# Masking by a product, plain float32 products for eight chunks, and value means on TensorE, in a fused attention and two-layer expert kernel

## The chip, the cores and the metric

The kernel runs on one core of a Trainium2 chip. The metric is the device time of one execution in microseconds (us); the time of a kernel is the median of its runs.

## What is computed

Three stages follow one another. The first is attention over two batches, eight heads, 768 positions and 64 channels per head. Each position sees the neighbours nearer than 16 positions and, besides, one summary per block of 32 positions (24 of them): the elementwise maximum of the keys and the mean of the values. The second stage is a dense layer pair with an ELU between, 512 to 2048 to 512. The third sends each of the 1536 tokens to one of eight experts.

```python
k_sum = k.reshape(B, H, nb, block, D).max(axis=3)
v_sum = v.reshape(B, H, nb, block, D).mean(axis=3)
scores_l = scale * np.matmul(q, k.transpose(0, 1, 3, 2))
mask_l = np.abs(pos[:, None] - pos[None, :]) < window
scores_s = scale * np.einsum('bhsd,bhnd->bhsn', q, k_sum) + np.log(block)
scores_all = np.concatenate([np.where(mask_l, scores_l, -1e9), scores_s], axis=-1)
...
h = x @ w_in
g = np.where(h > 0.0, h, np.exp(np.minimum(h, 0.0)) - 1.0)
x = g @ w_out
...
out[mask] = gate_w[mask, None] * eom[mask, e, None] * (np.maximum(x[mask] @ w1[e], 0.0) @ w2[e])
```

## The kernel before

**Units and blocks.** The 1536 tokens are 24 attention units of 64 positions; units 0 to 11 are batch 0, the rest batch 1. The units form four blocks of 8, 4, 6 and 6 units, so 512, 256, 384 and 384 tokens (`UNITS`, `TBS`). The dense layers run block by block. Within a block the 2048 hidden features are 16 chunks of 128 (`NF`). Chunk c of a block consists of `mm_h` (twelve products into one PSUM bank), `elu`, and two chunks later `mm_y`, which adds its share to the block's output banks, one per 128 tokens (`TPB`).

**One attention unit.** Four pairs of heads share a unit. `scores` (line 303) makes, for each pair, a product of 128 rows (64 queries of two heads) by 120 columns (24 summaries and 96 neighbours). `maxes` (line 312) adds the mask to each pair's scores and takes the row maximum in one VectorE instruction of its own kind per pair (line 319), followed by a read of the accumulator; the masked scores lie in SBUF as `e`. `at1b` takes the exponentials on ScalarE, from `e` to `e`, with the maximum as bias. In units 3 and 5 (`EXD`) `less_max` subtracts the maximum first, on GpSimd in unit 3 and on VectorE in unit 5, and one exponential serves all four pairs. `norm`, `turn` (four transposes), `weighted` (the product with the values), `x_hi` and `at5` follow and leave the unit's columns of x in a high and a low float32r part. The scores of units 0 to 7 take a bank of the pool with tag `y`, later ones the single bank `S`; transposes and weighted sums of the later units share the single bank `T`.

**Split products.** Float32 accuracy is kept by splitting operands into two float32r parts: three products (high by high, high by low, low by high) replace one. For `mm_y`, `split_w` (line 169) splits the weights with a ScalarE cast and a VectorE subtraction (line 176), and `split_g` (line 438) does the same to the ELU's output (`gh`, line 445, and `gl`, line 446). The first `C3` chunks of block 0 do without: there one plain float32 product is made per output bank.

**Weights.** The dense weights arrive as raw 64-bit words, 16 chunks of each matrix. `conv_t` (lines 138, 139, VectorE), `conv_r` (line 127, ScalarE) and `conv_f` (line 146, GpSimd) turn a piece into float32; pieces of `w_in` are split afterwards by `conv_h` (line 152, ScalarE) and `conv_l` (line 157, mostly VectorE). Each piece holds two buffers of the five-buffer pool `stg` meanwhile. All 32 conversions belong to block 0, two to a chunk in program order.

**Value means of batch 1.** Eight pieces of the transposed values are loaded into `stg` buffers (line 217), and GpSimd adds 32 neighbours in a tree of five steps per piece (`tree`, lines 233 to 237). `vsums2` (line 243) then transposes the 24 means on TensorE, through the bank `T`, and the result goes into the first 24 rows of every value tile of batch 1 (`v_pad`, line 255). For batch 0, `mean_v0` does this with products from the start.

**What sets the order.** The start, units 0 to 7 and the first chunks, follows the list `START`, in which each letter is a step and each number a unit or a chunk; what is loaded first follows `ORDER`. Behind it the program writes steps with due half-steps (`at(...)`), and the compiler's scheduler interleaves them on each engine by its own estimate of times; the expert stage has a planner of its own. On the chip each engine takes its instructions in that fixed order.

```python
for n, name in enumerate(("kT", "vT")):
    for p in range(NP):
        for hf in range(2):
            hs = SUM0 + 4 * n + p
            at(hs - 1, self.load_sum, name, p, hf)
            at(hs, self.red_sum, name, p, hf)
at(SUM0 + 9, self.vsums2)
...
self.mm_h(j, c, TB // 2 if j == 0 and c in self.half else 0)
conv()
self.split_w(j, c)
if i:
    self.split_g(*steps[i - 1])
self.elu(j, c)
```

Of the kernel before, what the change touches and what calls it, by code (L numbers as in the profile page):

```python
# [79 lines left out]
class Prog:  # L80
# [134 lines left out]
    def load_sum(self, name, p, hf):  # L215
        t = self.stg.tile([128, S // 2], F32, tag="stg", name="kst")
        self.nc.sync.dma_start(t, self.a[name][:, p, hf * S // 2:(hf + 1) * S // 2])
        self.st[name, p, hf] = t

    def red_sum(self, name, p, hf):  # L220
        nc = self.nc
        t = self.st.pop((name, p, hf)).rearrange("p (n w) -> p n w", w=32)
        n0, n1 = hf * NB // 2, (hf + 1) * NB // 2
        if name == "kT":
            nc.vector.tensor_reduce(self.ks[1][:, p, n0:n1], t, axis=AX.X, op=ALU.max)
            return
        if p == 0 and hf == 0:
# [2 lines left out]
        if p == NP - 1 and n1 == NB:  # L230
            nc.gpsimd.tensor_scalar(self.vs, self.vs, 1.0 / 32.0, None, op0=ALU.mult)

    def tree(self, p, n0, n1, t):
        nc = self.nc
        for w in (16, 8, 4, 2):
            nc.gpsimd.tensor_tensor(t[:, :, :w], t[:, :, :w], t[:, :, w:2 * w], op=ALU.add)
        nc.gpsimd.tensor_tensor(self.vs[:, p, n0:n1].unsqueeze(2), t[:, :, 0:1], t[:, :, 1:2], op=ALU.add)
# [1258 lines left out]
```

## Time and profile before

| | before |
|---|---|
| runs | 567.45, 567.43, 567.11 us |
| median | 567.43 us |
| profiled execution | 567.62 us, its span 565.4 us |
| TensorE busy in the span | 531.3 us (94%) |
| VectorE, ScalarE, GpSimd busy | 375.8, 317.3, 137.0 us |
| mean granted TensorE clock | 0.977 of full |

The span is the time from the first to the last instruction that the trace records; some 2.2 us of the execution lie outside it. PE is TensorE's products, PEld its weight loads, DVE is VectorE, ACT ScalarE, POOL GpSimd, SP the engine that issues most transfers. The attention start fills the first 40 us, block 0 the stretch from there to about 173 us (its last products overlap with the first of block 1), blocks 1 to 3 the stretch to about 380 us, the experts the rest. A float32 product stands in the trace as two matmul records, a float32r or bfloat16 product as one.

### The profile page before, as it was taken

How to read it: one execution, taken by the hardware profiler on the slowest of the kernel's cores; microseconds unless marked ns; L12 is line 12 of the kernel's file. 1: busy time of each engine (PE TensorE's matmuls, PEld its weight loads, DVE VectorE, ACT ScalarE, POOL GpSimd, SP SyncE). 2: the span in 40 equal slices, each digit the busy share in tenths (PEclk: the TensorE clock that was granted, in tenths of full speed). 3: DMA queues.
4: the chain of work that ended last, by engine and by line, in shares of the span. 5: the costliest groups of instructions: out<-in, count | busy, mean ns of one | idle time of the engine just before them, and what ended most of it. 6: DMA issues, size and time to landing. Idle time of an engine off the chain costs nothing. (4 is left out here: it accounts for less than half of the span.)

```text
span 565.4 us, 9609 instructions
## 1 busy us (share of the span) xinstructions
PE 531.3 (94%) x3089; PEld 422.0 (75%) x3089; DVE 375.8 (66%) x978; ACT 317.3 (56%) x774; POOL 137.0 (24%) x180
## 2 busy tenths in 40 slices
PE   8777997889869999999999999999999999999995
PEld 4465675667659889988888988987888665675884
DVE  7999999999966887687656779785841100444510
ACT  5774666756447877776566755673232222555620
POOL 3656245325980000000000000431431111100001
PEclk9999998999889999999999999998999999999999
DMA  9999543242133130310100101531077989494611
GB/s 289 329 362 394 187 156 124 86 116 79 43 105 122 48 94 16 108 57 14 48 2 0 57 1 39 170 128 57 7 206 278 373 280 362 168 373 130 234 69 40
DMA packets 39003, 81.33 MB, mean 144 GB/s; under 512 B 4128, under 2 KB 9632, under 8 KB 38945
## 3 DMA queue, kind: packets, MB, share of 16 engines
q1 hardware_dynamic: 36624, 73.30, 38.4%
q0 software_dynamic: 2320, 7.34, 3.7%
q8 instruction: 26, 0.43, 0.3%
q14 instruction: 33, 0.26, 0.2%
HBM read 103.70 MB, written 6.55 MB: 195 GB/s over the span
## 5 line engine op out<-in xcount | busy, mean ns | idle before, releaser
L422 PE MATMUL h<-xh,wi 128*128 128x384 f32 (+2 forms) x528 | 145.3, 343 | 3.0 <-ACT wi L152 1.9
L465 PE MATMUL y<-wsp,gh 128*128 128x512 f32 x368 | 116.0, 403 | 6.1 <-DVE wsp L176 5.9
L422 PEld LDWEIGHTS h<-xh,wi 128*128 128x128 f32 x528 | 95.3, 192 | 11.5 <-ACT wi L152 2.4
L422 PE MATMUL h<-xl,wi 128*128 128x384 f32 (+2 forms) x264 | 89.2, 338 | 0.0
L465 PEld LDWEIGHTS y<-wsp,gh 128*128 128x128 f32 x368 | 66.7, 190 | 20.1 <-DVE wsp L176 7.6
L465 PE MATMUL y<-wsp,gl 128*128 128x512 f32 x184 | 69.8, 399 | 0.0
L1153 DVE TENSOR_TENSOR holdl<-S,holdh 128x512 fp32r<-128x512 f32 x22 | 15.2, 689 | 72.1 <-ACT holdh L1149 53.7
L1121 PE MATMUL h<-w2s,holdh 128*128 128x512 f32 x176 | 60.9, 407 | 0.0
L1164 PE MATMUL y<-w2s,holdh 128*128 128x512 f32 x176 | 59.1, 398 | 0.0
L422 PEld LDWEIGHTS h<-xl,wi 128*128 128x128 f32 x264 | 50.8, 192 | 3.9 <-issue 0.2
L176 DVE TENSOR_TENSOR wsp<-wo,wsp 128x512 fp32r<-128x512 f32 x62 | 47.4, 765 | 8.1 <-ACT wsp L175 7.5
L175 ACT CAST wsp<-wo 128x512 fp32r<-128x512 f32 x62 | 38.2, 619 | 21.6 <-PE y L465 14.5
L434 DVE SCALAR_TENSOR_TENSOR elt<-ele,elt 128x384 f32<-128x384 f32 (+2 forms) x64 | 38.7, 605 | 16.9 <-ACT ele L432 16.5
L445 ACT CAST gh<-elp 128x384 fp32r<-128x384 f32 (+2 forms) x62 | 31.5, 508 | 30.6 <-DVE elp L435 22.4
L431 ACT ACTIVATE elt<-h 128x384 f32<-128x384 f32 (+2 forms) x64 | 31.3, 490 | 24.1 <-PE h L422 20.0
L435 DVE SCALAR_TENSOR_TENSOR elp<-elt,elp 128x384 f32<-128x384 f32 (+2 forms) x64 | 41.9, 655 | 3.5
L446 DVE TENSOR_TENSOR gl<-elp,gh 128x384 fp32r<-128x384 f32 (+2 forms) x62 | 37.4, 602 | 7.7 <-ACT gh L445 7.3
L465 PEld LDWEIGHTS y<-wsp,gl 128*128 128x128 f32 x184 | 34.4, 189 | 7.6 <-DVE gl L446 0.6
L1121 PEld LDWEIGHTS h<-w2s,holdh 128*128 128x128 f32 x176 | 33.8, 192 | 8.4 <-issue 0.8
L1164 PEld LDWEIGHTS y<-w2s,holdh 128*128 128x128 f32 x176 | 33.0, 188 | 8.4 <-issue 1.6
L336 ACT ACTIVATE e<-e,nb 128x120 f32<-128x120 f32 x88 | 33.7, 388 | 8.7 <-DVE nb L324 8.6
L1121 PE MATMUL h<-w2s,holdl 128*128 128x512 f32 x88 | 35.0, 398 | 0.0
(290 smaller groups left out, 948.0 us busy)
## 6 DMA issues: line engine op xcount, KB each, us to landing
wo<-in_w SPq DMA_DIRECT2D x9, 2048.0 KB
wo<-in_w SPq DMA_DIRECT2D x18, 1024.0 KB
ri<-in_w_in SPq DMA_DIRECT2D x16, 512.0 KB
ro<-in_w_out SPq DMA_DIRECT2D x16, 512.0 KB
wo<-in_w SPq DMA_DIRECT2D x32, 256.0 KB
w2p<-in_w SPq DMA_DIRECT2D x32, 256.0 KB
w2q<-in_w SPq DMA_DIRECT2D x24, 256.0 KB
q<-in_q SPq DMA_DIRECT2D x18, 256.0 KB
```

Of the source, the lines that this page charges most:

```text
L175: nc.scalar.copy(w[:, 0], f)
L176: nc.vector.tensor_tensor(w[:, 1], f, w[:, 0].bitcast(F32), op=ALU.subtract)
L336: nc.scalar.activation(e[:, p], e[:, p], AF.Exp, bias=nb[:, p:p + 1], scale=0.125, accum_out=sm[:, p:p + 1])
L422: nc.tensor.matmul(h, lhsT=w[:, wl, k * 128:k * 128 + 128], rhs=x[:, k, a:b], start=(n == 0), stop=(n == 11))
L431: nc.scalar.activation(t, h, AF.Tanh, scale=0.5)
L434: nc.vector.scalar_tensor_tensor(t, e, 1.0, t, op0=ALU.add, op1=ALU.mult)
L435: nc.vector.scalar_tensor_tensor(p, t, 0.0, p, op0=ALU.min, op1=ALU.add)
L445: nc.scalar.copy(gh, p)
L446: nc.vector.tensor_tensor(gl, p, gh.bitcast(F32), op=ALU.subtract)
L465: nc.tensor.matmul(self.y[j][t], lhsT=gx[:, sl], rhs=wx, start=(c == 0 and n == 0), stop=(c == NF - 1 and n == len(ops) - 1))
L1121: nc.tensor.matmul(self.h[s, hf], lhsT=x[:, k], rhs=w, start=(n == 0), stop=(n == 11))
L1164: nc.tensor.matmul(self.y2[s], lhsT=g[:, ks], rhs=w, start=(i == 0 and n == 0), stop=(i == 7 and n == 2))
```

## The change

There are three parts. **Mask.** The mask becomes the first product of a unit's accumulation group: a bfloat16 product of `mq` (two 64 by 64 identities side by side, and three rows of ones) with `mk` (the mask's rows, and the constant of the summaries in three bfloat16 parts), 480 columns wide; the four score products add to it. VectorE then takes one plain maximum over the four pairs, `at1b` reads the scores from PSUM, and `less_max` is on VectorE for both units. The bank of the scores is now held until the exponentials are done. The mask and the constants are loaded ahead of three of the four key tiles; `mask_parts` builds `mq` on GpSimd and `mk` on VectorE. **Second product.** `C3` goes from 2 to 8: eight chunks of block 0 have plain float32 products in `mm_y` and no splits. Their ELU output takes the buffers of `gh` and `gl`. **Value means.** Six pieces of the untransposed values of batch 1 are loaded, and each is reduced by four float32 products with four columns (`blk`) into the bank `T`, which ScalarE copies to `vs`.

```diff
-C3 = 2
+C3 = 8
-ORDER = "k3 k1 k2 k0 q2 q0 q5 q3 v7 c0 n1 c1 n4 n0 q1 ...
+ORDER = "k3 c1 c0 k1 k2 k0 q2 q0 q5 q3 v7 n1 n4 n0 q1 ...
-EXP = (0, 1, 2, 3, 4, 6, 7)
...
     def load_c(self, i):
+        nc.sync.dma_start(self.mask[:MK], self.a["mask"])
+
+    def mask_parts(self):
+        nc = self.nc
+        self.mq = self.const.tile([128, 128], BF16, name="mq")
+        self.mk = self.const.tile([128, 3, NK], BF16, name="mk")
+        nc.gpsimd.memset(self.mq[UQ:MK], 1.0)
+        for h in range(2):
+            nc.gpsimd.tensor_copy(self.mq[:UQ, h * UQ:h * UQ + UQ], self.ident[:UQ, :UQ])
+        nc.vector.tensor_copy(self.mk[:MK], self.mask[:MK])
...
+    def load_v1(self, i):
+        t = self.stg.tile([128, 512], F32, tag="stg", name="vn1")
+        self.nc.sync.dma_start(t, self.a["vn1"][i])
+        self.st["v", i] = t
+
+    def mean_v1(self, i):
+        t = self.st.pop(("v", i))
+        if i == 0:
             self.vs = self.sm.tile([128, NP, NB], F32, tag="vs", name="vs", bufs=1)
-        self.tree(p, n0, n1, t)
...
+        T = self.bank(self.psa, "T")
+        for p in range(NP):
+            self.nc.tensor.matmul(T[:, 4 * p:4 * p + 4], lhsT=t[:, p * 128:p * 128 + 128], rhs=self.blk[:, 20:24], start=True, stop=True)
+        self.nc.scalar.copy(self.vs[:, :, 4 * i:4 * i + 4], T[:, :16].rearrange("p (a n) -> p a n", a=NP))
...
+        m = self.mk[:MK, 0 if u % UPB == 0 else (2 if u % UPB == UPB - 1 else 1)]
+        nc.tensor.matmul(ps, lhsT=self.mq[:MK], rhs=m.unsqueeze(1).to_broadcast([MK, NP, NK]), start=True, stop=False)
         for p in range(NP):
-            nc.tensor.matmul(ps[:, p], lhsT=s["q"][:, p], rhs=k, start=True, stop=True)
+            nc.tensor.matmul(ps[:, p], lhsT=s["q"][:, p], rhs=k, start=False, stop=(p == NP - 1))
...
-        for p in range(NP):
-            nc.vector.tensor_tensor_reduce(e[:, p], ps[:, p], m, scale=1.0, scalar=-3.0e38, op0=ALU.add, op1=ALU.max, accum_out=mx[:, p:p + 1])
+        nc.vector.tensor_reduce(mx, ps, axis=AX.X, op=ALU.max)
...
-            nc.scalar.activation(e[:, p], e[:, p], AF.Exp, bias=nb[:, p:p + 1], scale=0.125, accum_out=sm[:, p:p + 1])
+            nc.scalar.activation(e[:, p], ps[:, p], AF.Exp, bias=nb[:, p:p + 1], scale=0.125, accum_out=sm[:, p:p + 1])
...
-        (self.nc.gpsimd if u in EXP else self.nc.vector).tensor_tensor(s["e"], s["e"], s["mx"].unsqueeze(2).to_broadcast([128, NP, NK]), op=ALU.subtract)
+        self.nc.vector.tensor_tensor(s["e"], s["ps"], s["mx"].unsqueeze(2).to_broadcast([128, NP, NK]), op=ALU.subtract)
...
+        pool, tag = (self.gp, "gh" if c % 2 else "gl") if j == 0 and c < C3 else (self.el, "p")
+        p = pool.tile([128, TB], F32, tag=tag, name="elp")[:, :TBS[j]]
...
+        for i in range(6):
+            hs = SUM0 + 4 + 2 * i // 3
+            at(hs - 1, self.load_v1, i)
+            at(hs, self.mean_v1, i)
```

The scheduler also places other work anew. In the rows below line numbers of the changed kernel are larger by 14 to 19; a number behind `ri`, `ro` or `wi` is the weight chunk, `cv_t` a piece being converted, and each `elp` written from `elt` ends one chunk's ELU.

The first place is VectorE in chunk 7 of block 0, before, from the conversion of `ro10` to the end of the ELU (`elp_1224`) and one row on:

```order
L138 TENSOR_SCALAR cv_t_1209<-ro10_956 128x512
L446 TENSOR_TENSOR gl_1219<-elp_1146,gh_1218 128x512
L434 SCALAR_TENSOR_TENSOR elt_1222<-ele_1223,elt_1222 128x512
L324 TENSOR_SCALAR nb_1305<-mx_1300 128x4
L139 SCALAR_TENSOR_TENSOR cv_t_1209<-ro10_956,cv_t_1209 128x512
L138 TENSOR_SCALAR cv_t_1242<-ri11_1019 128x512
L435 SCALAR_TENSOR_TENSOR elp_1224<-elt_1222,elp_1224 128x512
L157 TENSOR_TENSOR wi10_1206<-cv_t_1175,wi10_1206 128x512
```

The same place in the changed kernel, from shortly behind the ELU of chunk 6 on (`elp_1146` ends chunk 7's):

```order
L153 SCALAR_TENSOR_TENSOR cv_t_1138<-ro10_932,cv_t_1138 128x512
L367 TENSOR_SCALAR rr_1110<-sm_1044 128x4
L152 TENSOR_SCALAR cv_t_1156<-ri11_980 128x512
L368 RECIPROCAL rr_1110<-rr_1110 128x4
L153 SCALAR_TENSOR_TENSOR cv_t_1156<-ri11_980,cv_t_1156 128x512
L375 TENSOR_TENSOR e_1039<-e_1039,rr_1110 128x480
L171 TENSOR_TENSOR wi10_1135<-cv_t_1104,wi10_1135 128x512
L152 TENSOR_SCALAR cv_t_1187<-ro11_982 128x512
L450 SCALAR_TENSOR_TENSOR elt_1144<-ele_1145,elt_1144 128x512
L152 TENSOR_SCALAR cv_t_1224<-ri12_984 128x512
L153 SCALAR_TENSOR_TENSOR cv_t_1187<-ro11_982,cv_t_1187 128x512
L451 SCALAR_TENSOR_TENSOR elp_1146<-elt_1144,elp_1146 128x512
```

`gl` is gone from the chunk, and four pieces are converted ahead of its ELU's end (`ro10`, `ri11`, `ro11`, and the first step of `ri12`), where the last one begun had been `ri11`.

The second place is VectorE behind the ELU of chunk 12 before (`elp_1602`), where the last two pieces are converted:

```order
L435 SCALAR_TENSOR_TENSOR elp_1602<-elt_1600,elp_1602 128x512
L138 TENSOR_SCALAR cv_t_1550<-ri15_1191 128x512
L176 TENSOR_TENSOR wsp_1665<-wo_101,wsp_1665 128x512
L139 SCALAR_TENSOR_TENSOR cv_t_1550<-ri15_1191,cv_t_1550 128x512
L446 TENSOR_TENSOR gl_1669<-elp_1602,gh_1668 128x512
L434 SCALAR_TENSOR_TENSOR elt_1672<-ele_1673,elt_1672 128x512
L435 SCALAR_TENSOR_TENSOR elp_1674<-elt_1672,elp_1674 128x512
L138 TENSOR_SCALAR cv_t_1587<-ro15_1255 128x512
```

In the changed kernel, from `gl` of chunk 10 to the end of the ELU of chunk 12 (`elp_1494`):

```order
L462 TENSOR_TENSOR gl_1402<-elp_1333,gh_1401 128x512
L152 TENSOR_SCALAR cv_t_1479<-ro15_1169 128x512
L450 SCALAR_TENSOR_TENSOR elt_1405<-ele_1406,elt_1405 128x512
L153 SCALAR_TENSOR_TENSOR cv_t_1479<-ro15_1169,cv_t_1479 128x512
L451 SCALAR_TENSOR_TENSOR elp_1407<-elt_1405,elp_1407 128x512
L190 TENSOR_TENSOR wsp_1485<-wo_101,wsp_1485 128x512
L190 TENSOR_TENSOR wsp_1553<-wo_101,wsp_1553 128x512
L419 TENSOR_TENSOR xl1_210<-T_1413,xh1_209 128x4x64
L462 TENSOR_TENSOR gl_1489<-elp_1407,gh_1488 128x512
L450 SCALAR_TENSOR_TENSOR elt_1492<-ele_1493,elt_1492 128x512
L451 SCALAR_TENSOR_TENSOR elp_1494<-elt_1492,elp_1494 128x512
```

The last piece (`ro15`) is converted ahead of the end of chunk 11's ELU (`elp_1407`), and none stands behind it; before, it stood behind the ELU of chunk 13.

The third place is TensorE at the change from block 0 to block 1, where `vs` (the means) is transposed. Before, in chunk 1 of block 1:

```order
L465 MATMUL y_848<-wsp_1718,gl_1792 128x512
L309 MATMUL S_1874<-k_1734,q_1733 128x120 x4
L422 MATMUL h_1893<-xh1_203,wi1_610 128x256
L422 MATMUL h_1893<-xl1_204,wi1_610 128x256
L422 MATMUL h_1893<-xh1_203,wi1_610 128x256 x2
L243 MATMUL T_1737<-c0_128,vs_1556 24x128 x4
L422 MATMUL h_1893<-xl1_204,wi1_610 128x256
L422 MATMUL h_1893<-xh1_203,wi1_610 128x256 x2
```

In the changed kernel, from the scores of unit 13 on; the product with `vn1` is the last of the six sets:

```order
L322 MATMUL S_1755<-mk_202,mq_201 128x480
L325 MATMUL S_1755<-k_1617,q_1616 128x120
L250 MATMUL T_1570<-c0_128,vn1_1538 128x4 x4
L325 MATMUL S_1755<-k_1617,q_1616 128x120 x3
L436 MATMUL h_1772<-xh1_209,wi1_600 128x256
```

and, after the other products of that chunk:

```order
L436 MATMUL h_1772<-xh1_209,wi1_600 128x256
L481 MATMUL y_830<-wsp_1669,gh_1720 128x512 x2
L481 MATMUL y_830<-wsp_1669,gl_1721 128x512
L257 MATMUL T_1620<-c0_128,vs_1448 24x128 x4
L481 MATMUL y_831<-wsp_1669,gh_1720 128x512 x2
```

The transposes moved from among that chunk's first products into the second products of chunk 15, and the unit's scores stand behind a product of `mk` and `mq` in the same bank.

## Rows read from the trace of the kernel before

**Rows 1.** The page, busy time of each engine

```profile
PE 531.3 (94%) x3089; PEld 422.0 (75%) x3089; DVE 375.8 (66%) x978; ACT 317.3 (56%) x774; POOL 137.0 (24%) x180
```

**Rows 2.** Stretches: start:end, length, busy of five engines, clock, DMA share, GB/s

```profile
0.00:20.00 20.00, 17.25 (x82) 9.46 (x83) 15.72 (x67) 12.92 (x48) 8.25 (x29) 1.00 0.95 304
80.00:100.00 20.00, 15.76 (x78) 12.01 (x78) 20.00 (x37) 12.36 (x30) 8.78 (x6) 0.91 0.34 113
140.00:160.00 20.00, 18.00 (x78) 14.17 (x77) 17.47 (x31) 10.45 (x25) 20.00 (x28) 0.91 0.27 83
160.00:180.00 20.00, 15.04 (x111) 13.62 (x110) 11.73 (x32) 11.22 (x34) 7.44 (x18) 0.83 0.25 82
200.00:250.00 50.00, 50.00 (x377) 44.95 (x376) 38.18 (x132) 35.65 (x109) 1.45 (x4) 1.00 0.23 73
```

**Rows 3.** Waits of PE, whole span: us in total, times, longest

```profile
PE y L465 <- DVE wsp L176: 5.9, 4, 1.8
```

**Rows 4.** DVE in order of time: start us, us, line, operation [idle before]

```profile
52.23 1.22 DVE L435 SCALAR_TENSOR_TENSOR elp<-elt,elp 128x512 f32<-128x512 f32 x1
...
62.88 0.68 DVE L176 TENSOR_TENSOR wsp<-wo,wsp 128x512 fp32r<-128x512 f32 x1
63.48 0.68 DVE L435 SCALAR_TENSOR_TENSOR elp<-elt,elp 128x512 f32<-128x512 f32 x1
...
69.11 0.42 DVE L138 TENSOR_SCALAR cv_t<-ri 128x512 int32<-128x512 int32 x1
...
78.66 1.52 DVE L138 TENSOR_SCALAR cv_t<-ro 128x512 int32<-128x512 int32 x1
...
135.21 0.68 DVE L435 SCALAR_TENSOR_TENSOR elp<-elt,elp 128x512 f32<-128x512 f32 x1
```

**Rows 5.** POOL in order of time, at 78 us

```profile
78.31 1.59 POOL L146 TENSOR_TENSOR cv_t<-cv_t,cv_r 128x512 int32<-128x512 int32 x1 [1.99 <-ACT gh L445]
```

**Rows 6.** PE in order of time, 61 to 83 us

```profile
61.58 3.59 PE L465 MATMUL y<-wo,elp 128*128 128x512 f32 x8
65.01 0.60 PE L371 MATMUL T<-c,e 128*120 128x128 f32 x4
65.45 1.05 PE L309 MATMUL S<-k,q 128*128 128x120 f32 x8
66.26 0.48 PE L422 MATMUL h<-xh,wi 128*128 128x512 f32 x1
...
70.53 0.69 PE L392 MATMUL T<-et,v 120*64 120x64 f32 x16
...
81.22 0.39 PE L465 MATMUL y<-wsp,gh 128*128 128x512 f32 x1
...
82.81 0.39 PE L465 MATMUL y<-wsp,gl 128*128 128x512 f32 x1
```

**Rows 7.** PE in order of time, 138 to 173 us

```profile
138.32 2.10 PE L465 MATMUL y<-wsp,gh 128*128 128x512 f32 x8
...
148.88 0.50 PE L422 MATMUL h<-xh,wi 128*128 128x512 f32 x1 [1.87 <-ACT wi L152]
...
167.06 1.03 PE L243 MATMUL T<-c,vs 128*24 128x128 f32 x4 [4.96 <-POOL vs L231]
...
172.91 0.28 PE L422 MATMUL h<-xh,wi 128*128 128x256 f32 x1
```

**Rows 8.** DVE in order of time: mask instructions of a unit, 67 us

```profile
67.30 0.27 DVE L319 CUSTOM_DVE_ANT_0 e<-S,mask 128x120 f32<-128x120 f32 x1
...
68.11 0.68 DVE L446 TENSOR_TENSOR gl<-elp,gh 128x512 fp32r<-128x512 f32 x1
```

**Rows 9.** DVE in order of time: sums of 480 elements

```profile
18.55 1.20 DVE L344 TENSOR_REDUCE sm<-e 128x4 f32<-128x480 f32 x2
```

**Rows 10.** PEld in order of time: warm-up, bfloat16, 512 columns

```profile
7.06 1.39 PEld L185 LDWEIGHTS <-z 128*128 128x128 bf16 x7 [0.20 <-issue]
```

**Rows 11.** ACT groups, 53.4 to 135.9 us: exponentials of attention

```profile
L336 ACT ACTIVATE e<-e,nb 128x120 f32<-128x120 f32 x16 | 6.1, 387 | 1.8 <-DVE nb L324 1.8
```

More of the change, by code (lines that the diff above doesn't have):

```diff
@@ L66 @@
 NTT = NT // 128
-FAR = -8.0e9
+FAR = -2.0 ** 33
+MK = UQ + 3
 KF = 11
@@ L213, in mean_v0, with load_sum, red_sum @@
         self.nc.tensor.matmul(self.V0[:NB], lhsT=self.blk[:, 20 - 4 * i:44 - 4 * i], rhs=self.vn[i], start=(i == 0), stop=(i == 5))
-    def load_sum(self, name, p, hf):
+    def load_sum(self, p, hf):
         t = self.stg.tile([128, S // 2], F32, tag="stg", name="kst")
[L217 to L227, printed above, removed]
-            self.vs = self.sm.tile([128, NP, NB], F32, tag="vs", name="vs", bufs=1)
-        self.tree(p, n0, n1, t)
[L230 to L237, printed above, removed]
+        self.nc.sync.dma_start(t, self.a["kT"][:, p, hf * S // 2:(hf + 1) * S // 2])
+        self.st[p, hf] = t
+    def red_sum(self, p, hf):
+        t = self.st.pop((p, hf)).rearrange("p (n w) -> p n w", w=32)
+        self.nc.vector.tensor_reduce(self.ks[1][:, p, hf * NB // 2:(hf + 1) * NB // 2], t, axis=AX.X, op=ALU.max)
+    def load_v1(self, i):
[5 more added lines that the diff above has]
+        if i == 0:
+            self.vs = self.sm.tile([128, NP, NB], F32, tag="vs", name="vs", bufs=1)
+        T = self.bank(self.psa, "T")
+        for p in range(NP):
+            self.nc.tensor.matmul(T[:, 4 * p:4 * p + 4], lhsT=t[:, p * 128:p * 128 + 128], rhs=self.blk[:, 20:24], start=True, stop=True)
+        self.nc.scalar.copy(self.vs[:, :, 4 * i:4 * i + 4], T[:, :16].rearrange("p (a n) -> p a n", a=NP))
     def vsums2(self):
@@ L569, in part1 @@
             f(int(x[1:]))
+        self.mask_parts()
         self.new_x(0)
@@ L601, in part1 @@
         rank = {"at4": 0, "at3": 1, "at2": 2, "at1": 3, "at1b": 4, "at5": 4}
-        for n, name in enumerate(("kT", "vT")):
-            for p in range(NP):
-                for hf in range(2):
-                    hs = SUM0 + 4 * n + p
-                    at(hs - 1, self.load_sum, name, p, hf)
-                    at(hs, self.red_sum, name, p, hf)
+        for p in range(NP):
+            for hf in range(2):
+                at(SUM0 + p - 1, self.load_sum, p, hf)
+                at(SUM0 + p, self.red_sum, p, hf)
+        for i in range(6):
+            hs = SUM0 + 4 + 2 * i // 3
+            at(hs - 1, self.load_v1, i)
+            at(hs, self.mean_v1, i)
         at(SUM0 + 9, self.vsums2)
@@ L1450, in arrays @@
     out["kw"] = f(kw[NS:])
-    out["vT"] = f(v.transpose(0, 1, 3, 2).reshape(B, NP, 128, S).transpose(0, 2, 1, 3)[1])
     vn = np.zeros((B, S + 32, H, D), v.dtype)
     vn[:, 16:-16] = v.transpose(0, 2, 1, 3)
-    out["vn"] = f(vn[0, 16:-16].reshape(6, 128, H * D))
+    out["vn"], out["vn1"] = (f(vn[b, 16:-16].reshape(6, 128, H * D)) for b in range(B))
     out["vw"] = f(np.stack([vn[:, u * UQ:u * UQ + WIN] for u in range(UPB)], 1).reshape(NU, WIN, H * D))
-    m = np.full((3, UQ, NK), FAR, np.float32)
+    m = np.zeros((3, MK, NK), np.float32)
     for t, u in enumerate((0, 1, UPB - 1)):
@@ L1459, in arrays @@
         j = u * UQ - 16 + np.arange(WIN)[None]
-        m[t, :, NB:][(abs(i - j) < 16) & (j >= 0) & (j < S)] = 0.0
-    m[:, :, :NB] = LN32X8
+        m[t, :UQ, NB:][(abs(i - j) >= 16) | (j < 0) | (j >= S)] = FAR
+    rest = np.full(1, LN32X8, np.float32)
+    for i in range(3):
+        part = (rest.view(np.uint32) & np.uint32(0xFFFF0000)).view(np.float32)
+        m[:, UQ + i, :NB] = part
+        rest = rest - part
     blk = np.zeros((128, 44), np.float32)
     blk[np.arange(128), 20 + np.arange(128) // 32] = 1.0 / 32.0
-    out["mask"] = f(np.concatenate([m, m], 1).transpose(1, 0, 2))
+    out["mask"] = f(m.transpose(1, 0, 2))
     out["c0"] = f(np.concatenate([np.eye(128, dtype=np.float32), blk], 1))
```

11 lines of the change are left out of this document (6 added, 5 removed).

## The prediction, made before the changed kernel ran

> **What bounds the kernel now.** I read the totals first, then the stretches, then what TensorE waits for, then the engines in order of time. TensorE is busy for 531.3 of 565.4 us [rows 1], but this is a mean over stages. From 200 to 250 us it has no gap, 50.00 of 50.00 us [rows 2], and I take blocks 1 to 3 to be like that. There whatever is added to TensorE lengthens the run, and whatever is taken off another engine is worth nothing. In block 0 VectorE is the bound: from 80 to 100 us it is busy for 20.00 of 20 us and TensorE for 15.76 [rows 2], and TensorE's waits for the split weights, 5.9 us in four, lie there [rows 3]. At the end of block 0 GpSimd takes over: 20.00 of 20 us from 140 to 160 [rows 2], most of it the tree of value sums, for whose result TensorE stands still for 4.96 us, after 1.87 us for a late weight chunk [rows 7]. So the change is judged in three stages: start and block 0 up to about 138 us (VectorE), 138 to 173 us (GpSimd), and everything later (TensorE).
>
> Prices on VectorE: a 128 by 512 operation on two float32 tensors costs 0.60 us (starts 62.88 and 63.48), a first conversion step at most 0.42; the same step takes 1.52 while GpSimd converts [rows 4, 5]. A conversion on GpSimd therefore holds VectorE up by 1.1 us, and a converted piece costs VectorE 0.42 + 0.60 + 1.1 = 2.1 us. I call chunk c's ELU done when its second VectorE instruction ends: chunk 0's at 53.4, chunk 11's at 135.8 us [rows 4].
>
> **Start.** Of the mask, four instructions with their reads took 0.81 us (67.30 to 68.11) [rows 8]. The plain maximum is not in the trace; its nearest row is the sum of as many elements, 0.60 us each [rows 9]; I take 0.60, with 0.5 to 0.8 as bounds, since no row takes a maximum from PSUM. Eight units save 0.21 each, and unit 8's mask falls behind chunk 0's ELU (0.8): 2.5 us less. Unit 3's subtraction comes over from GpSimd (0.60, as 480 elements) and the mask is cast once (0.42 or less, as a first conversion step of more elements): 1.0 more. VectorE is busy for 15.72 of the first 20 us [rows 2], so of these 1.5 us I count 1.2. In SP's queue 96 KB of mask and 88 KB of constants pass three key loads; at 304 GB/s [rows 2] the keys come 0.6 us later, and the first scores with them, but the masks they were to wait for anyway are there; GpSimd's two small copies fit into its waits for keys. I set this at 0 (0 to 0.8).
>
> **Block 0 to chunk 11.** Here the order decides, not the number of instructions removed. Counted between the ELUs of chunks 0 and 11 in the two orders, VectorE loses 5 weight splits and 6 `gl`: 11 x 0.60 = 6.6 us. But the scheduler brings conversions forward: 24 pieces stand there instead of 21, 10 `conv_l` instead of 9, 3 `xl` instead of 4. That is 3 x 2.1 + 0.6 - 0.4 = 6.5 us. The sum is -0.1, taken as 0. Bounds: -6, if the conversions hold VectorE for half of 1.1 us (24 x 0.55 = 13 less, of which TensorE lets half show), and +4, if pieces wait for the five `stg` buffers in chunks 5 to 8, where 14 of them now stand. TensorE pays for the six plain products: one chunk takes 3.43 us (61.58 to 65.01) instead of twelve at 0.227 (81.22 to 82.81 are seven), 2.72 us [rows 6]; 6 x 0.71 = 4.3 us, all under VectorE's bound. Its cover would be gone only if VectorE came 10 us earlier: by these prices TensorE alone could reach `mm_y` of chunk 11 at about 127 us (eight plain second products 27.4, eleven `mm_h` and three split second products 38.1, scores, transposes and weighted sums of three to four units at 0.81 + 0.44 + 0.69 and the first means 8, from 53 us). So chunk 11's ELU is done at 134.6. Behind it in VectorE's queue stand two weight splits, one `xl` and `gl` of chunk 11, 2.1 us; TensorE begins that chunk's second products a pair of products ahead of `gl`, at 136.3 instead of 138.32 us [rows 7]: **2.0 us gained**.
>
> **138 to 173 us.** Out go the two waits, 6.8 us [rows 7], and half-speed stretches behind them. The granted clock was 0.91 and 0.83 in these two stretches [rows 2], against 1.00 later. From 140 to 160 a share of 0.18 of the time stood at 1.2 GHz, 3.6 us, so 1.8 lost; from 167.06 to 172.91 [rows 7] stand four transposes (0.44), eight 256-column products (0.9) and twelve of 512 (2.72), 4.1 us at 2.4 GHz, so 1.7 lost. In go the means. 24 products with four columns are not in the trace: transposes of 128 columns cost 0.11 each (65.01 to 65.45), score products of 120 columns 0.20 (65.45 to 66.26, four in eight records) [rows 6], so a set costs 0.44 to 0.81; I take 0.5, nearer the lower, because four columns are fewer than either has: 3.0 us. Two units' mask products cost 0.5 (next part). One more half-speed spell follows TensorE's own wait for chunk 11: 0.9, as half of the losses above. Sum: -6.8 - 3.5 + 3.0 + 0.5 + 0.9 = **-5.9 us**. The loads of the values pass the same 1.57 MB through the same buffers, a GpSimd tree no longer holds those, and at 83 GB/s the queue is idle; I set them at 0 (up to 1 us, if the first comes late).
>
> TensorE's page of the Trainium skill ("TensorE: Matmul & The Clock Gate", section "Weight-path perf modes") says that the fast weight load does not serve float32 weights, and its section on LDWEIGHTS gives 107 ns for 128 columns. With two records to a float32 product, 48 x 0.107 = 5.1 us would be an estimate for the means, and the forecast 564.2. The score products at 0.10 us a record [rows 6] agree with it as a limit; no row here has so few columns.
>
> **After 173 us.** Ten units (14 to 23) put a bfloat16 product of 480 columns on a TensorE without gaps. The warm-up's loads, seven in 1.39 us [rows 10], give 0.21 us for 512 columns, so 0.19; the upper bound adds the 0.12 of a change of operand (0.48 - 0.39 at 66.26 and a little) [rows 6]. I take 0.25: **+2.5 us** (1.9 to 3.1). Relief of VectorE, ScalarE and GpSimd is worth 0 there.
>
> **Sum.** -2.0 - 5.9 + 2.5 = -5.4 against the profiled execution's 567.62 us, which is 0.2 above the median of the runs: 562.2, or 562.0 on the median's scale; I give **562.1 us**.
>
> **Rivals.** *TensorE bound throughout* (chance 0.20): the holds cost less than 1.1 us, VectorE keeps ahead, and TensorE reaches chunk 11 at 127 us. Gain 11.3, then 6.8 (no new spell at half speed), less 2.5: 15.6, so 552. For it: GpSimd's total work falls; against it: VectorE had not one idle microsecond from 80 to 100. *The means cost their weight loads* (0.12): 24 products with as many weight columns as the score products take 0.20 us each, whatever they stream; six sets cost 4.9 instead of 3.0 [rows 6], and the time is 564.0. For it: in the score products too a load stands before every record. Against it: transposes load the same weights in 0.11. *The freed time is taken back* (0.16): `stg` buffers, shared by conversions, keys and values, make chunk 11 four microseconds later, the first means come 1 us late: 567 - within the 0.2% (1.1 us) that a measurement of this kernel can tell from no change, or just beside. *The masks wait for ScalarE* (0.12): a score bank is now free after the exponentials, not after the maximum. In the order seven of the ten later mask products (units 14 to 20) carry a wait for ScalarE at the head of TensorE's queue, with `mm_h` and `mm_y` behind them. Four exponentials take 4 x 0.39 = 1.5 us [rows 11]. If ScalarE comes late by that much in each of the seven, 10.5 us are added: 572.6. From 0.8 us a unit on it eats the gain. Against it: scores stand four to five half-steps apart, and ScalarE is busy for 35.65 of 50 us there [rows 2].
>
> **How the numbers follow.** The forecast has 0.40. Its own bounds (-6 to +4, 0.44 to 0.81 a set, 1.9 to 3.1) give 556 to 566.5. Faster by over 0.2% are 0.39 of it, 0.20 of TensorE bound, 0.11 of the weight loads, 0.05 of the time taken back and 0.01 of the last: 0.76. Within: 0.01 + 0.01 + 0.09 + 0.01, 0.12. Slower: 0.02 + 0.10, 0.12. The range goes from 554, towards the TensorE case, to 567, which leaves out the slow case and most of the fast one.
>
> **What would show it.** No GpSimd tree and no wait of TensorE for `vs`; chunk 11's ELU done at 133 to 136 us, with TensorE's waits gathered in chunks 8 to 11 rather than spread; the last product of block 0 ending near 165 instead of 173; four sums in 0.4 to 0.8 us; 0.2 to 0.3 us for each mask product and no wait ahead of it after 173 us. An ELU of chunk 11 at 127 or at 139 us would make the forecast wrong, and so would TensorE's idle time in blocks 1 and 2.

## Result and the profile after

The changed kernel takes 572.31 us (median of four runs, 571.29 to 573.87) against 567.27 for the kernel before beside it: ratio 1.0089, 95% interval 1.0072 to 1.0106. It is slower, where 562.1 was forecast. The profiled execution took 571.91 us and has a span of 570.1.

The busy line and the stretches, which answer to [rows 1, 2]; the columns are those of [rows 2].

```profile
PE 538.5 (94%) x3137; PEld 424.4 (74%) x3137; DVE 361.6 (63%) x800; ACT 309.4 (54%) x768; POOL 116.1 (20%) x141
```

```profile
0.00:20.00 20.00, 13.14 (x58) 8.61 (x58) 9.38 (x19) 8.55 (x35) 6.62 (x30) 0.83 0.78 246
80.00:100.00 20.00, 18.02 (x91) 10.61 (x90) 19.93 (x25) 11.55 (x27) 11.13 (x8) 1.00 0.43 139
100.00:120.00 20.00, 13.09 (x53) 8.70 (x49) 19.97 (x30) 10.66 (x24) 9.79 (x7) 0.83 0.39 123
140.00:160.00 20.00, 18.03 (x85) 14.66 (x84) 12.11 (x18) 10.70 (x24) 2.40 (x2) 0.91 0.13 40
160.00:180.00 20.00, 20.00 (x127) 17.64 (x126) 10.95 (x24) 9.80 (x29) 0.96 (x2) 1.00 0.17 47
200.00:250.00 50.00, 50.00 (x393) 45.07 (x393) 37.34 (x108) 37.38 (x122) 1.26 (x4) 1.00 0.21 66
```

VectorE lost 14 us of work and GpSimd 21, as meant, and GpSimd is gone from 140 to 160 us. But in the first 20 us every engine did less than before, and from 100 to 120 TensorE stood still for 7 us at a lowered granted clock (0.83). In the kernel before that stretch read:

```profile
100.00:120.00 20.00, 16.58 (x86) 12.81 (x86) 20.00 (x38) 12.88 (x31) 8.53 (x6) 1.00 0.30 91
```

TensorE's longest waits after say where:

```profile
PE T L385 <- DVE xl L419: 7.4, 2, 6.9
PE y L325 <- POOL ks L214: 3.9, 1, 3.9
...
PE T L250 <- DVE xl L419: 2.0, 1, 2.0
...
PE y L322 <- DVE mk L123: 1.8, 1, 1.8
```

Two of them (3.9 and 1.8) are of the start, and the largest, 6.9, is in block 0. The waits for `wsp` [rows 3] and for `vs` [rows 7] are gone.

**The start.** SP's, VectorE's and TensorE's queues of the kernel after, in order of time:

```profile
1.66 0.33 SPq L113 DMA_DIRECT2D mask<-in_mask  x1
2.04 1.29 SPq L204 DMA_DIRECT2D kT<-in_kT  x3
3.38 2.33 SPq L281 DMA_DIRECT2D qn<-in_q  x4
9.07 0.33 SPq L300 DMA_DIRECT2D v<-in_vw  x1
```

```profile
9.07 0.34 DVE L123 CAST mk<-mask 67x360 bf16<-67x360 f32 x1 [4.17 <-DMA mask<-in_mask]
...
12.14 0.95 DVE L208 TENSOR_REDUCE qk<-kT 128x24 f32<-128x768 f32 x1 [0.31 <-DMA kT<-in_kT]
```

```profile
9.47 0.36 PE L322 MATMUL y<-mk,mq 67*128 67x480 bf16 x1 [1.77 <-DVE mk L123]
13.74 2.04 PE L325 MATMUL y<-qk 128*128 128x120 f32 x8 [3.90 <-POOL ks L214]
...
45.97 0.39 PE L436 MATMUL h<-xh,wi 128*128 128x256 f32 x1
```

The mask's load, 94 KB, was issued at 1.66 us, and the cast that waits for it started at 9.07. The three key loads behind it came late too: the last reduction of keys starts at 12.14 us. The same three points in the kernel before:

```profile
7.78 0.95 DVE L194 TENSOR_REDUCE qk<-kT 128x24 f32<-128x768 f32 x1 [0.34 <-DMA kT<-in_kT]
```

```profile
9.38 3.80 PE L309 MATMUL y<-qk 128*128 128x120 f32 x32 [0.42 <-POOL ks L200]
...
39.97 0.39 PE L422 MATMUL h<-xh,wi 128*128 128x256 f32 x1
```

The first scores come 4.36 us later, and then at half the speed (eight records in 2.04 us, 32 in 3.80 before; the granted clock from 10 to 20 us is 0.66, 1.00 before). At the first `mm_h` product 6.00 us are lost. The last ELU of block 3 is 6.51 us late (second instruction at 387.31, 380.80 before), the span 4.7 us longer; where the 1.8 us behind that ELU, mostly in the experts' stage, come back was not followed up.

**Block 0.** From the first `mm_h` product to the last second product of block 0, of the kernel before and then of the kernel after:

```profile
39.97:173.10 133.13, 113.44 (x561) 87.72 (x559) 122.25 (x213) 79.50 (x178) 73.50 (x80) 0.94 0.43 144
```

```profile
45.97:179.16 133.19, 118.90 (x591) 87.06 (x588) 113.56 (x168) 74.54 (x174) 51.51 (x40) 0.96 0.41 134
```

Block 0 is as long as it was. TensorE is busy 5.46 us more and idle 5.40 less (19.69 to 14.29); the wait for the tree of value means alone was 4.96. Without it and the 1.87 for `wi` [rows 7], 12.9 us of idle time were there before and 14.3 are there now, although VectorE has 8.7 us less to do.

### The profile page after: what moved, and what is told of

The parts are those of the page before. It is cut to its first block, busy times and chain, and to the rows that moved or that the text cites. A ratio compares the mean times of both kernels' runs of the same rounds, so it can differ in the third digit from the quotient of the medians.

```text
span 570.1 us, 9476 instructions
## 1 busy us (share of the span) xinstructions
PE 538.5 (94%) x3137; PEld 424.4 (74%) x3137; DVE 361.6 (63%) x800; ACT 309.4 (54%) x768; POOL 116.1 (20%) x141
## 5 line engine op out<-in xcount | busy, mean ns | idle before, releaser
L481 PE MATMUL y<-wsp,gh 128*128 128x512 f32 x320 | 99.5, 403 | 0.0
L481 PEld LDWEIGHTS y<-wsp,gh 128*128 128x128 f32 x320 | 58.7, 191 | 10.2 <-ACT gh L461 0.3
L481 PE MATMUL y<-wsp,gl 128*128 128x512 f32 x160 | 60.9, 402 | 0.0
L450 DVE SCALAR_TENSOR_TENSOR elt<-ele,elt 128x384 f32<-128x384 f32 (+2 forms) x64 | 40.3, 630 | 24.4 <-ACT ele L448 23.6
L190 DVE TENSOR_TENSOR wsp<-wo,wsp 128x512 fp32r<-128x512 f32 x56 | 41.8, 751 | 11.3 <-ACT wsp L189 11.0
L189 ACT CAST wsp<-wo 128x512 fp32r<-128x512 f32 x56 | 35.1, 627 | 19.5 <-PE y L481 17.6
L461 ACT CAST gh<-elp 128x384 fp32r<-128x384 f32 (+2 forms) x56 | 28.1, 502 | 22.4 <-DVE elp L451 17.3
L462 DVE TENSOR_TENSOR gl<-elp,gh 128x384 fp32r<-128x384 f32 (+2 forms) x56 | 29.9, 535 | 9.1 <-ACT gh L461 8.9
L311 POOL COPY k<-ks 128x96 f32<-128x96 f32 x16 | 7.5, 473 | 138.0 <-PE S L325 122.8
L1183 PE MATMUL y<-w2s,holdl 128*128 128x512 f32 x88 | 34.4, 390 | 0.0
```

The costliest lines, as they stand in the source:

```text
L189: nc.scalar.copy(w[:, 0], f)
L190: nc.vector.tensor_tensor(w[:, 1], f, w[:, 0].bitcast(F32), op=ALU.subtract)
L450: nc.vector.scalar_tensor_tensor(t, e, 1.0, t, op0=ALU.add, op1=ALU.mult)
L461: nc.scalar.copy(gh, p)
L462: nc.vector.tensor_tensor(gl, p, gh.bitcast(F32), op=ALU.subtract)
L481: nc.tensor.matmul(self.y[j][t], lhsT=gx[:, sl], rhs=wx, start=(c == 0 and n == 0), stop=(c == NF - 1 and n == len(ops) - 1))
```

## The experiments

All ratios are to the kernel before, run on the same chip at the same time. Medians in us. The theories A to I are defined in the expectations, which were written before each run.

| run | what | median | ratio (95%) |
|---|---|---|---|
| e1 | after, mask load 80 rows | 568.73 | 1.0034 (1.0015-1.0053) |
| e2 | after, 67 rows behind the keys | 573.14 | 1.0104 (1.0086-1.0122) |
| e12 | after, mask load 72 rows | 565.98, one run | - |
| e3 | before, 8 plain chunks | 573.1 | 1.0078 (1.0044-1.0112) |
| e4 | e3 and means on TensorE | 566.98 | 0.9997 (0.9979-1.0014) |
| e6 | before, means on TensorE | 563.9 | 0.9937 (0.9914-0.9961) |
| e7 | before, mask product, 80 rows | 569.48 | 1.0043 (1.0018-1.0068) |
| e5 | e7 and means | 563.44 | 0.9920 (0.9892-0.9948) |
| e8 | e1 with 4 plain chunks | 567.75 | 0.9994 (0.9970-1.0018) |
| e11 | e1 with 1 plain chunk | 569.01 | 1.0038 (1.0015-1.0061) |
| e9 | e5, 32 warm-up products | 570.19 | 1.0056 (1.0037-1.0075) |
| e10 | e9, keys ahead of the mask | 568.92 | 1.0028 (1.0011-1.0045) |
| e13, e14 | e1, 26 and 28 warm-up products | 567.56, 568.93 | 1.0007 (0.9985-1.0029), 1.0030 (1.0006-1.0054) |
| e15 | e5, 26 warm-up products | 565.75 | 0.9976 (0.9957-0.9994) |
| e16 | before, 28 warm-up products | 569.21 | 1.0036 (1.0020-1.0052) |
| e17 | e1, `xl` from a copy | 567.53 | 0.9996 (0.9983-1.0010) |
| e18 | e5, `xl` from a copy | 566.68 | 0.9980 (0.9965-0.9995) |

**The start: e1, e12, e2.** e1 and e12 change two lines of the changed kernel (72 for 80 in e12); the order of every engine stays the same, so that nothing but the load differs.

```diff
-        nc.sync.dma_start(self.mask[:MK], self.a["mask"])
+        nc.sync.dma_start(self.mask[:80], self.a["mask"])
...
-    m = np.zeros((3, MK, NK), np.float32)
+    m = np.zeros((3, 80, NK), np.float32)
```

e2 moves the constants and the 67-row load behind the keys (`ORDER = "k3 k1 k2 k0 c1 c0 q2 ..."`); its order behind the start is a slightly different one.

> Only the mask's load differs from the changed kernel: 80 rows (13 of zeros behind the 67, never read), so 19% more bytes at the same place of SP's queue; the order of every engine is the same. Theory A (the shape of that load is what costs: its 67 rows keep it under way from 1.7 to about 9 us and the three key loads behind it with it): the mask lands by 5 us, the last keys by about 8.5 us instead of 12.1, the first scores start at 9.5 to 10.5 us instead of 13.7, at the full clock, the first mm_h product at 40 to 42 instead of 46.0 us, and the time is 566.5 to 569.0. Theory B (bytes ahead of the keys cost, whatever their shape): 18 KB more change nothing or make it worse: first scores at 13.7 us or later, 572 to 574. Theory C (the start's loss is absorbed later, block 0 ends when another engine lets it): first scores at about 10, but block 0's last second product still near 179 us and 571 to 573.

> The changed kernel with 72 rows of mask loaded (5 of zeros, never read). If it is the number of rows being no multiple of 16 that keeps the load under way: as the changed kernel, mask landing at 8 to 9 us, first scores at 13 us or later, 571 to 574. If only an odd number such as 67 does it: as e1, mask by 5, first scores near 10 us, 567 to 570.

> The changed kernel with constants and the 67-row mask loaded behind the four key loads. Theory A (the 67-row load holds up what stands behind it): the keys land as in the kernel before (4.2 to 7.8 us), the mask some 7 us after its issue, near 10 us, the query loads behind it late as well; first scores at 10 to 11 us, 568 to 571. Theory B (only the place ahead of the keys costs): keys on time, mask by 8.5, first scores at 9.5 us, 565 to 568. Theory C (the start does not matter): 571 to 573.

e1's casts and first products, VectorE then TensorE:

```profile
5.05 0.42 DVE L123 CAST mk<-mask 67x360 bf16<-67x360 f32 x1
```

```profile
10.05 1.12 PE L325 MATMUL y<-qk 128*128 128x120 f32 x8 [1.88 <-POOL ks L214]
...
40.13 0.39 PE L436 MATMUL h<-xh,wi 128*128 128x256 f32 x1
```

With more bytes in the load, the cast waits for nothing at 5.05 us, scores start at 10.05 at full speed, and `mm_h` 5.84 us earlier. The second VectorE instruction of chunk 0's ELU starts at 51.23 instead of 57.09 us, that of the last chunk of block 3 at 381.74 instead of 387.31: the lead of the start passes almost whole through three hundred microseconds. Of it 4.2 us are left in the spans and 3.6 us in the medians. e12 does the same (first `mm_h` at 40.41, cast at 5.09); its one run took 566.0 us, less than either of its ranges. In e2 the keys are on time, but the mask, issued at 3.08 us, holds the cast until 12.36:

```profile
12.36 0.34 DVE L123 CAST mk<-mask 67x360 bf16<-67x360 f32 x1 [3.61 <-DMA mask<-in_mask]
```

So it is neither bytes nor place, it is a load of 67 rows (theory A, for 67; that rows must be a multiple of 16 fell with e12). e2's time is outside A's range all the same, 573.1 us for 568 to 571, since the mask came at 12.4 and not near 10 us; theory C, for which the start doesn't matter, is refuted by e1 and not by e2. The Trainium skill, "DMA: Bandwidth & Descriptors", section "Why a DMA increments its semaphore by 16 and not by 1", has a rule that fits: a load is spread over the largest number of engines, up to 16, that divides the size of the slowest dimension on both of its sides, here the count of rows; 67, a prime, would go to one, 72 to twelve, 80 to sixteen. The times agree with it (7.4 us for 67 rows, at most 3.4 for 72 and for 80); no trace here shows the engines one by one.

**The parts alone: e3, e4, e6, e7, e5.** Each takes whole parts of the change over into the kernel before: `C3 = 8` and the ELU's buffers (e3), with `load_v1`/`mean_v1` (e4), these alone (e6), `mask_parts`/`scores`/`maxes` with 80 rows (e7), both of the latter (e5).

> The kernel before with the float32 second product for eight chunks instead of two, and nothing else (ELU results of those chunks in the gl and gh buffers). The prediction's step on block 0: ELU of chunk 11 one to two us earlier than 135.8, the wait for the value tree on GpSimd stays and takes the gain back: 565 to 567.5. Rival (what costs is the conversions brought forward, behind which xl stands in VectorE's queue): TensorE waits 4 to 7 us for xl in chunks 7 to 9, chunk 11's second products at 141 us or later instead of 138.3: 569 to 573.

> The kernel before with eight plain chunks and value means on TensorE, without any of the mask's part. Theory A (the start's 6 us and the later mask products' 2.1 us, ten at 0.21, are the mask's, the rest gains): 572.3 - 6.0 - 2.1 + 1.2 (relief of VectorE lost) = 565.4, 563 to 567. The prediction's own steps without the mask: 567.6 - 2.0 - 5.9 = 559.7, with means at 0.81 a set 561.6. Rival (plain chunks or means are the loss): 570 to 574.

> The kernel before with the value means on TensorE alone. Out go the wait of 4.96 us for the tree and the 1.87 us wait beside it, in come six sets at 0.81 (4.9 us), of which those that stand in waits for VectorE cost nothing. Theory D: 562 to 565.5 (less than e4, which has the plain chunks too, 567.0). Theory E (means cost what they save): 566 to 569, no better than e4.

> The kernel before with the mask's part alone, its load made 80 rows. Ten later mask products at 0.21 add 2.1 us to a TensorE without gaps; in the start nothing; in block 0 VectorE's relief (0.2 us for each unit) goes into TensorE's wait for the value tree, which stays. Theory A: 568 to 570.5. Rival (bank of scores is free only after the exponentials, so that mask products wait): 571 or more, with waits ahead of the mask products. Rival (VectorE's relief counts): 565 to 567.

> Mask by a product with the 80-row load and means on TensorE, but two plain chunks as in the kernel before. Theory D (the eight plain chunks are the second loss: conversions brought forward, ScalarE's next piece held for a stg buffer with xh behind it, xl behind the pieces on VectorE): TensorE's wait for xl ahead of transposes at most 2.5 us, chunk 11's second products at 136 to 139 us, no wait for a value tree: 563 to 566. Theory E (plain chunks help as predicted, and it is mask and means that cost: ten mask products at 0.21 and six sets at 0.81, 7 us): splits return to VectorE and the time rises from 568.7 to 570 to 573.

Means on TensorE gain in each of three pairs: 3.8 us (before to e6), 6.1 (e3 to e4), 6.0 (e7 to e5). In the traces the last second product of block 0 ends 4.4, 6.3 and 5.7 us earlier in these pairs, and the wait for `vs` (5.0, 7.0 and 5.5 us) is gone.

The mask costs 1.8 us in e7, within the range expected, but not for the reason expected: its first scores ran at about half speed after an idle time of 2.60 us (the second eight records in 1.90 us, at a granted clock of 0.83 from 10 to 20 us) and its first `mm_h` product is 2.47 us late (42.44 for 39.97), and behind block 0 its trace is no longer than that of the kernel before (392.2 for 392.3 us).

Eight plain chunks lose in e3, where I expected a small gain; 573.1 us is at the upper end of the rival's 569 to 573. Its runs spread from 568.1 to 574.6, and the profiled one (574.2) lost 1.7 us up to `mm_h` (41.63), where no plain chunk has yet run: its first 32 score records took 5.43 us after an idle time of 2.12, for 3.80 before. So not all of e3's loss is the plain chunks', nor all of the 6.1 us from e3 to e4 the means'.

e5 has the lowest median and is faster than both kernels; it is the change with the mask's 80 rows and without its six further plain chunks. e6, the means alone, can't be told from it (563.9, and the intervals overlap). TensorE's waits in e3, then e5, from 40 to 185 us:

```profile
PE T L243 <- POOL vs L231: 7.0, 1, 7.0
PE T L371 <- DVE xl L405: 5.5, 2, 4.4
```

```profile
PE h L436 <- DVE wi L171: 5.3, 4, 1.9
...
PE T L385 <- DVE xl L419: 0.5, 1, 0.5
```

**How many plain chunks: e8, e11.** `C3 = 4` and `C3 = 1` for 8 in e1.

> As e1, but four plain chunks instead of eight. Theory D: the conversions run ahead less; the wait for xl in chunks 7 and 8 shrinks below 4 us; 564 to 567. Theory E: between e1 (568.7) and what two plain chunks give, which it puts above e1: 569 to 571.

> e5 with one plain chunk instead of two. Theory D (every plain chunk costs TensorE 0.71 us and moves no bound): 562 to 564, same or a little below e5 (563.4). Rival (below two VectorE's splits decide again): 565 to 568.

With 8, 4, 2 and 1: 568.7, 567.8, 563.4, 569.0. e8 lies between the ranges of its two theories and e11 above both of its own. This is no trend, so e5 against e1 doesn't price a chunk. Something else changes from text to text.

**The order: e9, e10, e13 to e16.** The scheduler lays the loop behind the start out along a timeline that it simulates; `WARM = 26` to `32` for 22 shifts that timeline, and another order of the same work comes out.

> e5 with 32 warm-up products instead of 22: the ten more (3.4 us for 14 in e1) run in the gap of 2.73 us that TensorE had before its first scores in e5, after which the first 16 score products ran at half speed (1.72 and 1.90 us for eight instead of 1.05) and the granted clock of 10 to 20 us was 0.83. Theory F (that gap costs the clock, and with it the 2 us by which e5's first mm_h product at 42.1 was behind e1's 40.1): clock 1.00 up to 20 us, first mm_h product at 40 to 41 us, time 561 to 562.5. Rival (mm_h waits for other work, the clock of the start is not on the path): 563 to 565.

> e9 with constants and the 80-row mask loaded behind the four keys. Keys land at 4.2 to 7.8 us as in the kernel before, mask near 8.5: first scores at 9.3 to 9.8 us instead of 10.3; 0.5 us off e9 if the start decides. Rival (the cast of the mask stands behind the reductions and the query loads come later by as much): same as e9 or up to 1.5 us more.

> e1 with 26 warm-up products instead of 22; the four (about 1 us) run in the 1.88 us that TensorE waits before its first scores, so the start is e1's; behind it the scheduler writes another order of block 0. Theory D (plain chunks' own price, in any order): 568 to 570, with TensorE's wait for xl or one of its size in block 0. Theory G (the order that the scheduler happens on is worth more than any part of the change): off e1's 568.7 by 2 us or more, up or down, with the largest wait of block 0 at another place.

> e1 with 28 warm-up products, a third order of the same work. As for e13: theory D 568 to 570; theory G off e1 or off e13 by 2 us or more.

> e5 (two plain chunks) with 26 warm-up products; its gap before the first scores was 2.73 us and shrinks to some 1.7, so the start may gain up to 2 us as in e9. Theory D: 561.5 to 564. Theory G: 565 to 570, as e9 with its 570.2.

> The kernel before with 28 warm-up products: its warm-up ended 0.42 us ahead of the first scores, so six more put the scores off by about 1 us, and the order of block 0 is another. Theory D says nothing but that 1 us: 567.3 to 569. Theory G: the order of the kernel before is a lucky or an unlucky one too, 563 to 566 or 570 to 574.

e9 filled its gap as meant (clock 1.00 up to 20 us, first `mm_h` at 41.10 for 42.07) and was 6.8 us slower: theory F's start was right, its sum wrong, because the loop had another order. Two plain chunks have now taken 563.4, 565.8 and 570.2 us in three orders, eight 568.7, 567.6 and 568.9. Theory G holds for two plain chunks; for eight the orders lie within 1.4 us (e13 falls between the ranges of D and G) and theory D can't be refuted. e15 starts better than e5 (first `mm_h` at 39.65) and is 2.3 us slower. The kernel before is 1.9 us slower in its other order, between D's range and the slower of G's, of which the start explains nothing (`mm_h` at 39.72). e10 against e9: 1.3 us less, about the width of the intervals. The stretch of block 0 in e5, and in e9:

```profile
42.07:168.59 126.52, 114.26 (x611) 90.01 (x608) 116.55 (x177) 80.13 (x185) 54.90 (x40) 0.99 0.42 146
```

```profile
41.10:175.16 134.06, 118.71 (x615) 93.96 (x612) 122.02 (x180) 80.47 (x186) 51.97 (x40) 0.94 0.41 143
```

Of 7.54 us between them 3.09 are idle time and 4.45 are busy time for the same products, at a lower granted clock (0.94 against 0.99). e9's longest waits in it are 3.4 and 3.1 us, e5's 1.9. The 6.8 us are of the medians. The profiled run of e5 is the slowest of its six and that of e9 the fastest, and their spans are only 2.6 us apart: behind block 0 e9's was 1.9 us shorter up to the last ELU of block 3 (207.9 for 209.8) and 2.1 us shorter from there (184.1 for 186.2). The two traces show where block 0 differs, not the whole of the medians.

**The wait for `xl`: e17, e18.** In seven traces with eight plain chunks the transposes' wait for `xl` is the longest of block 0 apart from `vs`: 6.9 us (after, e1, e12), 5.9 (e14), 4.6 (e13), 4.4 (e3, e4). In e2 it came in three pieces, 5.9 us together. In the kernel before it was at most 2.1. In the kernel after, TensorE, ScalarE and VectorE there:

```profile
113.69 1.11 PE L385 MATMUL T<-c,e 128*120 128x128 f32 x4 [6.91 <-DVE xl L419]
```

```profile
107.19 0.67 ACT L141 ACTIVATE cv_r<-ri 128x512 int32<-128x512 uint32 x1 [2.11 <-DVE wi L171]
108.28 0.36 ACT L412 CAST xh<-T 128x256 fp32r<-128x256 f32 x1
```

```profile
105.40 1.75 DVE L171 TENSOR_TENSOR wi<-cv_t,wi 128x512 fp32r<-128x512 f32 x1
...
109.56 1.74 DVE L153 SCALAR_TENSOR_TENSOR cv_t<-ri,cv_t 128x512 int32<-128x512 int32 x1
111.22 0.68 DVE L171 TENSOR_TENSOR wi<-cv_t,wi 128x512 fp32r<-128x512 f32 x1
111.83 1.48 DVE L152 TENSOR_SCALAR cv_t<-ro 128x512 int32<-128x512 int32 x1
113.23 0.41 DVE L419 TENSOR_TENSOR xl<-T,xh 128x256 fp32r<-128x256 f32 x1
```

`xh` stands on ScalarE behind `cv_r`, a step of a conversion, which waits until VectorE has finished with a `stg` buffer; `xl` stands behind conversions on VectorE, 4.6 us after `xh` ended, and the next unit's transposes need the one bank that `xl` still reads. e17 and e18 free that bank earlier, with one ScalarE copy for each unit of block 1:

```diff
-        self.nc.scalar.copy(self.x[j][0][:, :, o:o + UQ], self.u[u]["O"])
+        O = self.u[u]["O"]
+        self.nc.scalar.copy(self.x[j][0][:, :, o:o + UQ], O)
+        if j == 1:
+            c = self.mask.rearrange("p a b -> p (a b)")[:, :256].rearrange("p (a q) -> p a q", a=NP)
+            self.nc.scalar.copy(c, O)
+            self.u[u]["O"] = c
```

> e1 with one more ScalarE copy (128x256, 0.37 us as xh) for each of the four units of block 1, into the mask's float32 buffer, which is no longer read; xl is computed from the copy, so the transposes' bank is free after ScalarE's two instructions and not after VectorE's queue. In e1 xh ended at 102.8 and xl at 107.7 us. Theory H (the wait for xl takes the plain chunks' gain): no wait of transposes for xl, the wait of 6.9 us at most 2.5 (for xh or its copy), chunk 11's second products at 138 to 140 us instead of 142.9, 563.5 to 566. Theory I (VectorE is late anyway, and TensorE meets it next at elp, wsp or gl): the waits only change their names, 567 to 570.

> The same copy in e5 (two plain chunks), where transposes waited 0.5 us for xl. Theory H: nothing to gain, 563 to 566 with the spread that other orders of e5 showed. Theory I: the same, so e17 against e18 shows what eight plain chunks are worth without that wait: by H e17 is at most 1 us above e18, by I 3 us or more.

e1's stretch of block 0, and e17's waits and stretch:

```profile
40.13:173.29 133.16, 118.72 (x591) 86.88 (x588) 113.61 (x168) 74.32 (x173) 52.14 (x40) 0.96 0.44 148
```

```profile
PE T L385 <- ACT mask L416: 4.3, 1, 4.3
PE T L385 <- DVE e L375: 3.2, 1, 3.2
```

```profile
40.77:170.58 129.81, 117.02 (x591) 86.61 (x588) 113.11 (x168) 75.03 (x178) 51.20 (x40) 0.99 0.44 151
```

The waits changed their names (theory I): ScalarE's copy is itself 4.3 us late, and the units' normalized exponentials `e` come 3.2 us late from VectorE. Of idle time 14.44 (e1) became 12.79, of time 1.2 us were won, and since e17's order is another than e1's too, this can't be put down to the copy. e18, where there was nothing to win, came out 3.2 us above e5, in yet another order and above its range. Against each other e17 and e18 differ by 0.85 us, which was the sign of theory H (at most 1 us) and not of I (3 or more): the two signs contradict each other, and neither theory is shown. What eight plain chunks cost by themselves stays open: over four orders each, 567.5 to 568.9 for eight and 563.4 to 570.2 for two. Shown is that no order of eight was measurably faster than the kernel before.

## Why the prediction was wrong, step by step

By the spans, the changed kernel came out 10.1 us above the forecast (570.1 for 565.4 less 5.4): 4.2 from the start (e1 to the kernel after), 6.5 up to chunk 11's second products and 1.6 from there to the end of block 0 (both in e1), less 2.2 that the stages behind did not take.

- **Start: wrong.** It holds 3.6 of the 5.0 us by which the change is slower. I set the key loads' delay "at 0 (0 to 0.8)", from bytes at 304 GB/s. It was 4.36 us at the first scores and 6.00 at `mm_h`, because the load had 67 rows. The bytes alone were priced well: in e1, with more of them, the first scores come 0.67 us later than before (10.05 for 9.38), where the bytes gave 0.6 and 0 was counted. So was the relief of VectorE: in e1 the second instruction of chunk 0's ELU starts at 51.23 instead of 52.23 us [rows 4], 1.0 us for 1.2 forecast.
- **Block 0 to chunk 11: wrong.** Two sentences failed: VectorE's sum "is -0.1, taken as 0", and TensorE's extra 4.3 us "all under VectorE's bound". The second VectorE instruction of the ELU in chunks 4 and 8, before and then in e1, and the start of chunk 11's second products in e1:

```profile
76.86 0.68 DVE L435 SCALAR_TENSOR_TENSOR elp<-elt,elp 128x512 f32<-128x512 f32 x1
...
113.09 0.68 DVE L435 SCALAR_TENSOR_TENSOR elp<-elt,elp 128x512 f32<-128x512 f32 x1
```

```profile
69.69 1.77 DVE L451 SCALAR_TENSOR_TENSOR elp<-elt,elp 128x512 f32<-128x512 f32 x1
...
115.06 0.68 DVE L451 SCALAR_TENSOR_TENSOR elp<-elt,elp 128x512 f32<-128x512 f32 x1
```

```profile
142.86 1.05 PE L481 MATMUL y<-wsp,gh 128*128 128x512 f32 x2
```

  In e1 the ELUs did run ahead, by 7.2 us in chunk 4, and were 2.0 behind in chunk 8. Chunk 11's ELU ends at 137.2, for 134.6 forecast, and its second products start at 142.9, for 136.3. Counting instructions between two ELUs missed which instruction of a queue another engine waits for; the place of `xl` and `xh` behind the conversions wasn't looked at. That TensorE waits there for 6.9 us is in the trace; that the time would be won without this wait is not shown (e17), so what else holds the loop back stays open. And the plain products were not covered: the stretch of block 0 is TensorE's busy time plus 12 to 17 us of idle time in all kernels with the means; e1 is busy 4.46 us longer than e5. That agrees with 6 x 0.71, though e9 shows that the clock can do as much.
- **138 to 173 us: right, but for the means' price.** From chunk 11's second products to the end of block 0 the kernel before took 34.78 us and e1 30.43: 4.35 less, for 5.9 forecast. A set of means takes 0.81 us:

```profile
158.38 0.95 PE L250 MATMUL T<-c,vn 128*128 128x4 f32 x8
159.19 0.49 PE L481 MATMUL y<-wsp,gh 128*128 128x512 f32 x1
...
172.35 0.38 PE L322 MATMUL S<-mk,mq 67*128 67x480 bf16 x1
172.56 0.38 PE L325 MATMUL S<-k,q 128*128 128x120 f32 x2
```

  0.5 was taken; six sets are 1.9 us more, which leaves 4.0. The rival on weight loads had this price exactly, 0.10 us for each of eight records whatever they stream. The prediction's 107 ns, from the Trainium skill ("TensorE: Matmul & The Clock Gate", section on LDWEIGHTS), is close to it.
- **After 173 us: right in the price, not in the stage's length.** A mask product takes 0.21 us (172.35 to 172.56), 2.1 for ten, for 2.5 forecast. But from the end of block 0 to the end of the trace the kernel before took 392.3 us, the kernel after 390.9, e1 392.6 and e7 392.2. That whatever is added to TensorE there lengthens the run is not borne out to the microsecond; what gave the 2.1 us back was not followed up.
- **The maximum from PSUM** took 0.57 us from its start to the next (77.24 to 77.81), for 0.60 taken.
- **Rivals.** "TensorE bound throughout" (552) fell: TensorE is idle for 14.44 us of block 0 in e1. "The masks wait for ScalarE" gave 572.6, close to the result, and was wrong all the same: no mask product behind 173 us waits. The number came in the main from the start, so the closeness is chance. "The freed time is taken back" named the `stg` buffers, which are in the chain of the 6.9 us, and was too small. That the load's shape could hold up the keys was no rival of mine at all.
